# Opening of a fused Fourier-mixing and ELU kernel: which queue brings the filter, and which the weights

## The chip, the cores and the metric

The kernel runs on one core of one Trainium2 chip. The metric is the device time of one execution in microseconds, the median of several runs. Before the change it was 2671.48 us (three runs, 2666.98 to 2671.87).

## The reference

Two blocks follow each other. The first mixes the sequence by a filter in the frequency domain, the second is a two-layer feed-forward with ELU:

```python
# x (8, 3008, 256); filt_r, filt_i (1505, 256); float32
X = np.fft.rfft(x, axis=1)
y = np.fft.irfft(X * (filt_r + 1j * filt_i)[None], n=3008, axis=1).astype(np.float32)
# w_in (256, 2048), w_out (2048, 256): float64
h = y.reshape(24064, 256) @ w_in
g = np.where(h > 0, h, np.exp(np.minimum(h, 0)) - 1)
out = (g @ w_out).astype(np.float32)
```

## The kernel before, in words

**The transform.** The length is 3008 = 47 x 64. For each of the eight batches the transform goes through 64-point stages (`a_unit`, with twiddle tables `ta`), 47-point stages (`b_unit`, table `gb`), a product with the filter on VectorE (L320 to L323), and the way back: 47 points (`bi_unit`, tables `gr` and `gi`) and 64 points (`n_unit`, tables `tn`). Between stages the data goes through DRAM (`z`, `yd`) so that another axis comes to lie on the partitions. `bi_unit` works on eight groups of frequencies, g = 0 to 7; its results are written to `yd` by `y_write` and read again by `y_read`.

**The feed-forward.** `up_steps` and `down_steps` multiply with blocks of the weights, combined in the manner of Strassen and Winograd with seven products instead of eight; `combine` (L394 to L397) makes the sums of the activations on VectorE. One item is a batch, one of six row groups m and one of four quarters q of the 2048 hidden units. These items fill TensorE for most of the span. While items of one batch run, the transform of the next one is laid in between by a plan of places (`plan`, `at`).

**The order of the work** is written by hand (`manual_schedule`): each engine runs its instructions in the order of the program text. Transfers issued by SyncE (`nc.sync`) go by one queue, those issued by GpSimd (`nc.gpsimd`) by another; on an engine whose instruction waits, all later ones wait too.

**The opening** (L641 to L720) is what the change is about. Batch 0 and the weights have no earlier work to hide behind, so this part has its own functions.

- `x_load_first(c)`, L232: for each of six chunks c, the upper half of x comes by SyncE's queue, the mirrored lower half by GpSimd's, and a piece of the forward table `tf` by SyncE's.
- `w_fetch(k)`, L554: the weights are float64, 16 pieces of 512 KB, all on GpSimd's queue. Pieces 4q and 4q+1 are of w_in, 4q+2 and 4q+3 of w_out. There is no room for all raw pieces at once: they lie in buffers that belong to the later pipeline or that the opening has used (6 to 9 in the tiles of x chunks 0 to 3, 10 and 11 in those of chunks 4 and 5, 12 to 14 in the buffers of pieces 1, 2 and 5, and 15 in that of piece 6).
- `w_split(k)` (VectorE), `w_float(k)` (four instructions on ScalarE) and `w_join(k)` (VectorE) make float32 values of the two 32-bit halves of each number. `w_join` of an odd piece also makes the four sums for the Strassen form (L618 to L621). `tick(k)` is `w_float(k)` and then `w_join(k - 1)`. Two sets of temporary tiles are used in turn.
- `a_first(c)`, L239: 16 matrix products and four copies by ScalarE for each chunk, with `w_split(c)` and `w_float(c)` ahead of them in the loop of L677.
- `t_first(g)`, L254: transposes on TensorE with the table `eye`, and copies by ScalarE. Groups 0 to 3 are done right behind the loop; the others in the loop of L695.
- `f_read_first(ff, c)`, L288: the filter in the order the products want, from rows 64 KB apart, in 11 transfers for each of the real and the imaginary part. Elements are 1 and 2 KB. The real part goes by SyncE's queue, the imaginary part by GpSimd's behind chunk 2 (L684). The tile `ff` holds all eight groups.
- The loop of L695: in step g the units `bi_unit(0, g - 2)` and `b_unit(0, g)`, and, if `TICKS` names a piece for the step, its `w_split` ahead of them and its `tick` behind:

```python
TICKS = {0: 7, 1: 8, 2: 9, 3: 10, 4: 11, 5: 12, 7: 13, 8: 14, 9: 15}
```

In the last step `y_write` and `y_read` bring the first row group, then come `w_join(15)` (L713), the loads of the next batch and `n_unit(0, 0)` (L720), from which the items start.

Of the kernel before, what the change touches and what calls it, by code (L numbers as in the profile page):

```python
# [25 lines left out]
P = 128  # L26
D = 256
# [13 lines left out]
def _make_tables():  # L41

    n2, k2 = np.arange(N2), np.arange(K2)
    ta, tn = np.zeros((P, H, P)), np.zeros((P, H, P))
    for i in range(H):
        for h in range(2):
            if h and i == 0:
                continue
            n1 = N1 - i if h else i  # L60
            th = 2 * np.pi * (((N1 * n2[:, None] + n1) * k2[None]) % N) / N
            c, s = np.cos(th), -np.sin(th)
            c[:, 0], s[:, 0] = 1.0, 1.0 - 2.0 * (n2 % 2)
# [36 lines left out]
    gf = np.zeros_like(gb)  # L100
    for o in (0, 64):
        gf[o:o + 48] = gb[o:o + 48].reshape(2, H, 2, 64).swapaxes(0, 1).reshape(48, 2, 64)
    return [t.astype(np.float32) for t in (ta, tn, gb, gr, gi, tf, np.eye(P), gf)]


def order(m):
# [5 lines left out]
def kernel(  # L112
# [8 lines left out]
):  # L121
    nc = tc.nc

    ta_d, tn_d, gb_d, gr_d, gi_d, tf_d, eye_d, gf_d = [
        nc.inline_tensor(t, name=n + "_t").ap()
        for t, n in zip(_make_tables(), ("ta", "tn", "gb", "gr", "gi", "tf", "eye", "gf"))
    ]

    def pool(name, bufs, **kw):
# [17 lines left out]
    psO = pool("psO", 1, space=PSUM)  # L147
    psM = pool("psM", 1, space=PSUM)

    gb, gr, gi = (glob.tile([P, 2, 64], FP32, name=n) for n in ("gb", "gr", "gi"))  # L150

    w_in, w_out = ([glob.tile([P, 7, 2, P], FP32, name="%s%d" % (n, i)) for i in range(4)] for n in ("wi", "wo"))

# [63 lines left out]
    def x_place_first(c):  # L217
        if c < XBUFS:
            t = xp.tile([P, 2, 2, D], FP32, tag="xc", name="xc").rearrange("p k u d -> p (k u) d")
        else:  # L220
            t = t1p.tile([P, XC, D], FP32, tag="t1", name="x1")
        if c < 2:
            w = tnp.tile([P, 4, P], FP32, tag="tn", name="tn")
        else:
            if c % 2 == 0:
                tas["pair"] = t4p.tile([P, 4, D], FP32, tag="t4", name="t0").rearrange("p u (w f) -> p (u w) f", f=P)
            w = tas["pair"][:, 4 * (c % 2):4 * (c % 2) + 4, :]
        xs[0, c], tas[0, c] = t, w
        if c == 0:
            nc.vector.memset(t[HALVES[1], 0, :], 0.0)  # L230

    def x_load_first(c):  # L232
        t = xs[0, c]
        u = 1 if c == 0 else 0
        nc.sync.dma_start(t[HALVES[0]].rearrange("p u d -> p (u d)"), raw(x, XC * c, [[N1 * D, 64], [1, XC * D]]))
        nc.gpsimd.dma_start(t[HALVES[1], u:XC, :], raw(x, N1 - XC * c - u, [[N1 * D, 64], [-D, XC - u], [1, D]]))
        nc.sync.dma_start(tas[0, c], tf_d[:, 4 * c:4 * c + 4, :])

    def a_first(c):  # L239
        xt, w = xs.pop((0, c)), tas.pop((0, c))  # L240
# [44 lines left out]
        for a, r in enumerate((LO, HI)):  # L285
            nc.gpsimd.dma_start(t[r].rearrange("p c u d -> p (c u d)"), fd[g, a].rearrange("q c u d -> q (c u d)"))

    def f_read_first(t, c):  # L288


        src, queue = ((filt_r, nc.sync), (filt_i, nc.gpsimd))[c]
        for a in ((0, 1), (1, 0))[c]:
            r = a * 64
            queue.dma_start(t[r:r + 48:2, :, c, :, :].rearrange("q g u d -> q g (u d)"),
                            raw(src, 2 * a, [[64 * D, 24], [4 * D, NG], [1, 2 * D]]))
            for u in range(2):
                g0 = 1 if a == u == 0 else 0
                for j, n in ((0, 16), (16, 7)):
                    queue.dma_start(t[r + 1 + 2 * j:r + 2 * (j + n):2, g0:NG, c, u, :],
                                    raw(src, 64 * (j + 1) - 4 * g0 - 2 * a - u,  # L300
                                        [[64 * D, n], [-4 * D, NG - g0], [1, D]]))
            if a == 0:
                queue.dma_start(t[1:48:2, 0, c, 0, :], raw(src, 32, [[64 * D, 24], [1, D]]))

    def tile_mm(ps, table, k, rhs, special):
        for u, w, v in ((0, 1, 1), (1, 1, 0)) if special else ((0, 2, 0),):
# [244 lines left out]

    wds = {}

    def w_fetch(k):  # L554
        q, j = divmod(k, 4)

        if k in (3, 4):
            wd = t2p.tile([P, 4, D], FP32, tag="t2", name="wd").rearrange("p u d -> p (u d)")
        elif k in (10, 11):
            wd = t1p.tile([P, XC, D], FP32, tag="t1", name="wd").rearrange("p u d -> p (u d)")  # L560
        elif k in (6, 7, 8, 9, 15):
            wd = xp.tile([P, 2, 2, D], FP32, tag="xc", name="wd").rearrange("p k u d -> p (k u d)")
        else:
            wd = fbufs[{5: 0, 12: 1, 13: 2, 14: 0}.get(k, k)].rearrange("p c u d -> p (c u d)")
        wd = wds[k] = wd.bitcast(U32).rearrange("p (a w) -> p a w", w=2)
        if j < 2:
            srcs = [moe_w_in.bitcast(U32)[ts(j, P), ts(q, 1024)]]
        else:
            srcs = [moe_w_out.bitcast(U32)[ts(4 * q + 2 * (j - 2) + i, P), :] for i in range(2)]
        for i, s in enumerate(srcs):  # L570
            n = 512 // len(srcs)
            nc.gpsimd.dma_start(wd[:, ts(i, n), :].rearrange("p a w -> p (a w)"), s)

# [67 lines left out]
    with tc.manual_schedule():  # L641


        TICKS = {0: 7, 1: 8, 2: 9, 3: 10, 4: 11, 5: 12, 7: 13, 8: 14, 9: 15}
        with tc.tile_pool(name="boot", bufs=1) as bp:
            ff = bp.tile([P, NG, 2, 2, D], FP32, name="ff")
            eye = bp.tile([P, P], FP32, name="eye")
            gf = bp.tile([P, 2, 64], FP32, name="gf")
            pq = [bp.tile([P, 2, D], FP32, name="pq%d" % i) for i in range(2)]
            zt[0] += [bp.tile([P, 16 * ROWS], FP32, name="zt%d" % i) for i in range(2)]  # L650

            for z in zt[0] + zt[1]:
                nc.gpsimd.memset(z.rearrange("p (k r) -> p k r", r=ROWS)[:, :, 48:64], 0.0)
            for c in range(NXC):
                x_place_first(c)
            for c in range(NXC):
                x_load_first(c)
                if c < 5:
                    w_fetch(c)
            nc.scalar.memzero(ff[:, 0:NG // 2])  # L660
            nc.vector.memset(ff[:, NG // 2:NG], 0.0)
            wtmp.append([kp.tile([P, 512], U32, tag=t, name=n) for t, n in (("k0", "wm"), ("k1", "we"))] +
# [3 lines left out]
                        [t1p.tile([P, XC, D], FP32, tag="t1", name="wfl").rearrange("p (a b) d -> p a (b d)", a=2)])  # L666
            for i, v in enumerate((1151.0 * 2 ** 23, 255.0 * 2 ** 23)):
                nc.vector.memset(edges[:, i:i + 1], v)
            for t, d in ((gr, gr_d), (gi, gi_d), (gf, gf_d), (eye, eye_d)):
                nc.sync.dma_start(t, d)  # L670
            f_read_first(ff, 0)

            def tick(k):
                w_float(k)
# [2 lines left out]
            for c in range(NXC):  # L677
# [2 lines left out]
                a_first(c)  # L680
                if c > 0:
                    w_join(c - 1)
                    w_fetch(c + 4)
                if c == 2:  # L684
                    f_read_first(ff, 1)
            for k in range(NXC + 4, 14):
                w_fetch(k)
            for g in range(4):
                t_first(g)
            w_split(NXC)  # L690
            tick(NXC)
            w_fetch(14)
            nc.sync.dma_start(gb, gb_d)
            tn_read(0, 0)
            for g in range(NG + 2):  # L695
                k = TICKS.get(g)
# [11 lines left out]
                    y_read(0, 0, (nc.sync, nc.scalar))  # L708
                if k:
                    tick(k)  # L710
                if g == 0:
                    w_fetch(15)
        w_join(15)  # L713
        for c in range(2):
            x_load(1, c)
# [102 lines left out]
```

## Time and profile before

The span of the profiled execution is 2667.6 us. From the page:

| engine | busy us | share |
|---|---|---|
| TensorE (PE) | 2597.2 | 97% |
| TensorE weight load (PEld) | 2209.1 | 83% |
| VectorE (DVE) | 1843.3 | 69% |
| ScalarE (ACT) | 1508.7 | 57% |
| GpSimd (POOL) | 248.0 | 9% |

Stretches of the opening, from the view of busy time by stage:

| us | PE busy | VectorE busy | ScalarE busy | TensorE clock | DMA share | GB/s |
|---|---|---|---|---|---|---|
| 10 to 30 | 10.97 | 11.43 | 15.44 | 0.83 | 1.04 | 286 |
| 34 to 48 | 8.75 | 6.20 | 9.75 | 0.76 | 1.03 | 172 |
| 50 to 60 | 0.00 | 0.77 | 2.53 | 0.50 | 1.05 | 284 |

Busy times are sums over the stretch. The clock is what the throttle granted TensorE, as a share of full speed, and the DMA share is the mean over the core's 16 DMA engines. In the traffic views, "q1 hardware_dynamic" is the queue of SyncE, "q0 software_dynamic" that of GpSimd; the columns are packets, MB and the time of the packets as a share of 16 engines' span. Each GpSimd transfer from the ninth on is issued only when the one eight before it has landed, so the timeline of its issues also tells landings. The last landings that VectorE's first product (L320, at 63.69 us) could have waited for are those of the filter.

### The profile page before, as it was taken

How to read it: one execution, taken by the hardware profiler on the slowest of the kernel's cores; microseconds unless marked ns; L12 is line 12 of the kernel's file. 1: busy time of each engine (PE TensorE's matmuls, PEld its weight loads, DVE VectorE, ACT ScalarE, POOL GpSimd, SP SyncE). 2: the span in 40 equal slices, each digit the busy share in tenths (PEclk: the TensorE clock that was granted, in tenths of full speed). 3: DMA queues.
4: the chain of work that ended last, by engine and by line, in shares of the span. 5: the costliest groups of instructions: out<-in, count | busy, mean ns of one | idle time of the engine just before them, and what ended most of it. 6: DMA issues, size and time to landing. Idle time of an engine off the chain costs nothing.

```text
span 2667.6 us, 37278 instructions
## 1 busy us (share of the span) xinstructions
PE 2597.2 (97%) x13508; PEld 2209.1 (83%) x13508; DVE 1843.3 (69%) x3203; ACT 1508.7 (57%) x2622; POOL 248.0 (9%) x300
## 2 busy tenths in 40 slices
PE   4799999999999999999999999999999999999998
PEld 3488789888898878988889878898789887898887
DVE  4876767677676776667766676676767677666665
ACT  5655555555555555555555555555555555555554
POOL 3031200012000120002100021001210011000000
PEclk7899999999999999999999999999999999999999
DMA  9464311443124331333214242134321333110110
GB/s 243 114 132 111 102 44 38 102 105 86 38 57 121 80 79 40 95 86 86 74 39 102 74 103 69 38 87 104 99 52 39 78 83 80 38 40 19 23 26 16
DMA packets 229832, 202.87 MB, mean 76 GB/s; under 512 B 132952, under 2 KB 196107, under 8 KB 229649
## 3 DMA queue, kind: packets, MB, share of 16 engines
q1 hardware_dynamic: 211889, 163.33, 24.9%
q0 software_dynamic: 17456, 36.70, 5.6%
q8 instruction: 107, 1.75, 0.3%
q14 instruction: 76, 0.62, 0.1%
q10 hardware_dynamic: 304, 0.46, 0.1%
HBM read 128.45 MB, written 74.97 MB: 76 GB/s over the span
## 4 chain that ended last, share of the span: by engine, by line
PE 94%; DVE 2%; DMA 2%; issue 1%; ACT 0%; SPq 0%; DVEq 0%
PE po L501 43%; PE phs L419 25%; PE phd L419 12%; PE pha L419 6%; PE psn L371 3%; PE pva L308 2%; PE psr L308 2%; PE psa L206 2%; DMA ff<-in_filt_r_dram 1%; DMA x<-in_x_dram 1%; DVE si L321 0%; DVE sr L320 0%; PE pvb L308 0%; DVE wfl L603 0%; DVE we L601 0%
## 5 line engine op out<-in xcount | busy, mean ns | idle before, releaser
L501 PE MATMUL po<-g,wo 128*128 128x256 f32 (+1 forms) x5376 | 1296.7, 375 | 0.0
L501 PEld LDWEIGHTS po<-g,wo 128*128 128x128 f32 x5376 | 1015.0, 190 | 129.5 <-issue 16.2
L430 ACT ACTIVATE g<-phs 128x512 f32<-128x512 f32 (+1 forms) x576 | 339.1, 589 | 842.8 <-PE phs L419 842.1
L427 DVE TENSOR_TENSOR g<-phd,g 128x512 f32<-128x512 f32 (+1 forms) x384 | 259.6, 676 | 463.8 <-ACT e L437 278.0
L437 ACT ACTIVATE e<-e 128x512 f32<-128x512 f32 (+1 forms) x768 | 477.3, 621 | 24.4
L419 PE MATMUL phs<-y,wi 128*128 128x256 f32 (+1 forms) x1536 | 394.8, 379 | 0.0
L419 PE MATMUL phs<-ys,wi 128*128 128x256 f32 (+1 forms) x1536 | 387.6, 375 | 1.5 <-ACT g L430 1.5
L441 DVE SCALAR_TENSOR_TENSOR g<-e,g 128x512 f32<-128x512 f32 (+1 forms) x576 | 387.1, 672 | 0.2 <-ACT e L437 0.2
L436 ACT ACTIVATE e<-g 128x512 f32<-128x512 f32 (+1 forms) x576 | 352.8, 612 | 35.4 <-DVE g L427 29.3
L419 PEld LDWEIGHTS phs<-y,wi 128*128 128x128 f32 x1536 | 284.5, 190 | 83.1 <-ACT t L340 34.1
L419 PEld LDWEIGHTS phs<-ys,wi 128*128 128x128 f32 x1536 | 291.4, 190 | 35.3 <-ACT g L430 2.2
L441 DVE SCALAR_TENSOR_TENSOR g<-e,phs 128x512 f32<-128x512 f32 (+1 forms) x192 | 129.9, 677 | 139.3 <-ACT e L437 139.3
L419 PE MATMUL phd<-ys,wi 128*128 128x256 f32 (+1 forms) x768 | 193.9, 375 | 1.8 <-DVE g L427 1.8
L419 PE MATMUL pha<-y,wi 128*128 128x256 f32 (+1 forms) x768 | 193.8, 375 | 0.0
L419 PE MATMUL phd<-y,wi 128*128 128x256 f32 (+1 forms) x768 | 193.7, 375 | 0.0
L436 ACT ACTIVATE e<-phs 128x512 f32<-128x512 f32 (+1 forms) x192 | 113.0, 588 | 141.6 <-PE phs L419 140.7
L329 POOL TENSOR_TENSOR sr<-sr,sp 128x512 f32<-128x512 f32 x56 | 71.2, 1272 | 1242.8 <-DVE sp L322 1242.8
L419 PEld LDWEIGHTS phd<-ys,wi 128*128 128x128 f32 x768 | 145.7, 190 | 18.9 <-DVE g L427 2.5
L419 PEld LDWEIGHTS pha<-y,wi 128*128 128x128 f32 x768 | 145.8, 190 | 16.8 <-ACT y L373 0.2
L419 PEld LDWEIGHTS phd<-y,wi 128*128 128x128 f32 x768 | 145.8, 190 | 16.5
L481 DVE TENSOR_TENSOR g<-g,g 128x512 f32<-128x512 f32 (+1 forms) x192 | 130.7, 681 | 6.7
L478 DVE TENSOR_TENSOR g<-g,g 128x512 f32<-128x512 f32 (+1 forms) x192 | 130.7, 681 | 6.6
(142 smaller groups left out, 2396.0 us busy)
## 6 DMA issues: line engine op xcount, KB each, us to landing
yd<-t SPq DMA_DIRECT2D x127, 192.0 KB
t<-yd SPq DMA_DIRECT2D x190, 128.0 KB
z<-t SPq DMA_DIRECT2D x84, 256.0 KB
f<-fd POOLq DMA_DIRECT2D x112, 192.0 KB, 3.7
t<-z SPq DMA_DIRECT2D x224, 96.0 KB
out_dram<-o SPq DMA_DIRECT2D x640, 32.0 KB
tn<-tn_t SPq DMA_DIRECT2D x48, 256.0 KB
xc<-in_x_dram SPq DMA_DIRECT2D x84, 128.0 KB
```

Source lines behind the costliest of these rows:

```text
L308: nc.tensor.matmul(ps[:, u:u + w, :], table[k, v, :], r[k, u:u + w, :], start=n == 0, stop=n == len(rhs) - 1)
L329: nc.gpsimd.tensor_tensor(out=sr, in0=sr, in1=p, op=ALU.add)
L371: nc.tensor.matmul(ps[:, ts(q, P)], t[:, i - 4 * m, ds(dh * P, P)], w[:, i - 4 * m, :], start=True, stop=True)
L419: nc.tensor.matmul(ps[:, a, 0:h], w_in[q][:, COMBO[n], a, :], y[n], start=start and a == 0, stop=True, skip_group_check=True)
L427: nc.vector.tensor_tensor(out=g[o], in0=i0, in1=i1, op=ALU.add)
L430: nc.scalar.activation(out=g[o], in_=i0, func=AXT.Copy)
L436: nc.scalar.activation(out=e, in_=src, func=AXT.Relu, scale=-1.0)
L437: nc.scalar.activation(out=e, in_=e, func=AXT.Exp, scale=-1.0)
L441: nc.vector.scalar_tensor_tensor(out=g[n], in0=es[n], scalar=1.0, in1=src, op0=ALU.subtract, op1=ALU.max)
L478: nc.vector.tensor_tensor(out=b12, in0=b22, in1=b12, op=ALU.subtract)
L481: nc.vector.tensor_tensor(out=g["t4"], in0=g["b21"], in1=g["t2"], op=ALU.subtract)
L501: nc.tensor.matmul(po[i][:, u, 0:h], w_out[q][:, COMBO[n], a, :], g[n][:, a, :], start=q == 0 and a == 0 and n in (1, 3, 6, 4), stop=True, ...
```

## The change

It rearranges what comes by which queue in the opening, and when. GpSimd's queue brings the lower half of x for all six chunks, then the whole filter, then weight pieces 8 to 15. SyncE's queue brings piece 0, the upper half of x with the tables `tf` and pieces 1 to 4 in between, the table `once` (which merges `eye` and `gf`), pieces 5 to 7, and the table `gs` (which merges `gb`, `gr` and `gi`). From chunk 2 on, `tf` is loaded for two chunks at a time. The conversions move as well: pieces 6 and 7 are both done ahead of the loop over the groups, 8 to 14 in steps 0, 1, 3, 5, 7, 8 and 9, and 15 behind it. It is meant to bring the filter before the products ask for it, and to take its small elements off SyncE's queue.

```diff
-    ta_d, tn_d, gb_d, gr_d, gi_d, tf_d, eye_d, gf_d = [
+    ta_d, tn_d, gs_d, tf_d, once_d = [
...
-    gb, gr, gi = (glob.tile([P, 2, 64], FP32, name=n) for n in ("gb", "gr", "gi"))
+    gs = glob.tile([P, 3, 2, 64], FP32, name="gs")
+    gb, gr, gi = (gs[:, i] for i in range(3))
...
-        nc.sync.dma_start(tas[0, c], tf_d[:, 4 * c:4 * c + 4, :])
+        if c < 2:
+            nc.sync.dma_start(tas[0, c], tf_d[:, 4 * c:4 * c + 4, :])
+        elif c % 2 == 0:
+            nc.sync.dma_start(tas.pop(("pair", c // 2)), tf_d[:, 4 * c:4 * c + 8, :])
...
-    def f_read_first(t, c):
-        src, queue = ((filt_r, nc.sync), (filt_i, nc.gpsimd))[c]
-        for a in ((0, 1), (1, 0))[c]:
-            r = a * 64
-            queue.dma_start(...)
+    def f_read_first(t):
+        for a, c in ((0, 0), (1, 1), (0, 1), (1, 0)):
+            r, src = a * 64, (filt_r, filt_i)[c]
+            nc.gpsimd.dma_start(...)
...
-    def w_fetch(k):
+    def w_fetch(k, queue=nc.gpsimd):
...
-        TICKS = {0: 7, 1: 8, 2: 9, 3: 10, 4: 11, 5: 12, 7: 13, 8: 14, 9: 15}
+        TICKS = {0: 8, 1: 9, 3: 10, 5: 11, 7: 12, 8: 13, 9: 14}
...
+            w_fetch(0, nc.sync)
             for c in range(NXC):
                 x_place_first(c)
             for c in range(NXC):
                 x_load_first(c)
-                if c < 5:
-                    w_fetch(c)
+                if 0 < c < 5:
+                    w_fetch(c, nc.sync)
...
-            for t, d in ((gr, gr_d), (gi, gi_d), (gf, gf_d), (eye, eye_d)):
-                nc.sync.dma_start(t, d)
-            f_read_first(ff, 0)
+            nc.sync.dma_start(once, once_d)
+            f_read_first(ff)
...
                 if c > 0:
                     w_join(c - 1)
-                    w_fetch(c + 4)
-                if c == 2:
-                    f_read_first(ff, 1)
+                    w_fetch(c + 4, nc.sync if c < 4 else nc.gpsimd)
+            nc.sync.dma_start(gs, gs_d)
             for k in range(NXC + 4, 14):
                 w_fetch(k)
             for g in range(4):
                 t_first(g)
-            w_split(NXC)
-            tick(NXC)
-            w_fetch(14)
-            nc.sync.dma_start(gb, gb_d)
+            for k in (NXC, NXC + 1):
+                w_split(k)
+                tick(k)
+                w_fetch(k + 8)
...
                 if k:
                     tick(k)
-                if g == 0:
-                    w_fetch(15)
+            w_split(15)
+            tick(15)
         w_join(15)
```

More of the change, by code (lines that the diff above doesn't have):

```diff
@@ L102, in _make_tables @@
         gf[o:o + 48] = gb[o:o + 48].reshape(2, H, 2, 64).swapaxes(0, 1).reshape(48, 2, 64)
-    return [t.astype(np.float32) for t in (ta, tn, gb, gr, gi, tf, np.eye(P), gf)]
+    once = np.stack([np.eye(P), gf.reshape(P, P)], 1)
+    return [t.astype(np.float32) for t in (ta, tn, np.stack([gb, gr, gi], 1), tf, once)]
 def order(m):
@@ L122 @@
     nc = tc.nc
-    ta_d, tn_d, gb_d, gr_d, gi_d, tf_d, eye_d, gf_d = [
+    ta_d, tn_d, gs_d, tf_d, once_d = [
         nc.inline_tensor(t, name=n + "_t").ap()
-        for t, n in zip(_make_tables(), ("ta", "tn", "gb", "gr", "gi", "tf", "eye", "gf"))
+        for t, n in zip(_make_tables(), ("ta", "tn", "gs", "tf", "once"))
     ]
@@ L225, in x_place_first @@
             if c % 2 == 0:
-                tas["pair"] = t4p.tile([P, 4, D], FP32, tag="t4", name="t0").rearrange("p u (w f) -> p (u w) f", f=P)
-            w = tas["pair"][:, 4 * (c % 2):4 * (c % 2) + 4, :]
+                tas["pair", c // 2] = t4p.tile([P, 4, D], FP32, tag="t4", name="t0").rearrange("p u (w f) -> p (u w) f", f=P)
+            w = tas["pair", c // 2][:, 4 * (c % 2):4 * (c % 2) + 4, :]
         xs[0, c], tas[0, c] = t, w
@@ L286, in f_read @@
             nc.gpsimd.dma_start(t[r].rearrange("p c u d -> p (c u d)"), fd[g, a].rearrange("q c u d -> q (c u d)"))
-    def f_read_first(t, c):
-        src, queue = ((filt_r, nc.sync), (filt_i, nc.gpsimd))[c]
-        for a in ((0, 1), (1, 0))[c]:
-            r = a * 64
-            queue.dma_start(t[r:r + 48:2, :, c, :, :].rearrange("q g u d -> q g (u d)"),
-                            raw(src, 2 * a, [[64 * D, 24], [4 * D, NG], [1, 2 * D]]))
+    def f_read_first(t):
+        for a, c in ((0, 0), (1, 1), (0, 1), (1, 0)):
+            r, src = a * 64, (filt_r, filt_i)[c]
+            nc.gpsimd.dma_start(t[r:r + 48:2, :, c, :, :].rearrange("q g u d -> q g (u d)"),
+                                raw(src, 2 * a, [[64 * D, 24], [4 * D, NG], [1, 2 * D]]))
             for u in range(2):
@@ L298, in f_read_first @@
                 for j, n in ((0, 16), (16, 7)):
-                    queue.dma_start(t[r + 1 + 2 * j:r + 2 * (j + n):2, g0:NG, c, u, :],
-                                    raw(src, 64 * (j + 1) - 4 * g0 - 2 * a - u,
-                                        [[64 * D, n], [-4 * D, NG - g0], [1, D]]))
+                    nc.gpsimd.dma_start(t[r + 1 + 2 * j:r + 2 * (j + n):2, g0:NG, c, u, :],
+                                        raw(src, 64 * (j + 1) - 4 * g0 - 2 * a - u,
+                                            [[64 * D, n], [-4 * D, NG - g0], [1, D]]))
             if a == 0:
-                queue.dma_start(t[1:48:2, 0, c, 0, :], raw(src, 32, [[64 * D, 24], [1, D]]))
+                nc.gpsimd.dma_start(t[1:48:2, 0, c, 0, :], raw(src, 32, [[64 * D, 24], [1, D]]))
     def tile_mm(ps, table, k, rhs, special):
@@ L571, in w_fetch @@
             n = 512 // len(srcs)
-            nc.gpsimd.dma_start(wd[:, ts(i, n), :].rearrange("p a w -> p (a w)"), s)
+            queue.dma_start(wd[:, ts(i, n), :].rearrange("p a w -> p (a w)"), s)
     wts, wtmp = {}, []
@@ L641 @@
     with tc.manual_schedule():
-        TICKS = {0: 7, 1: 8, 2: 9, 3: 10, 4: 11, 5: 12, 7: 13, 8: 14, 9: 15}
+        TICKS = {0: 8, 1: 9, 3: 10, 5: 11, 7: 12, 8: 13, 9: 14}
         with tc.tile_pool(name="boot", bufs=1) as bp:
             ff = bp.tile([P, NG, 2, 2, D], FP32, name="ff")
-            eye = bp.tile([P, P], FP32, name="eye")
-            gf = bp.tile([P, 2, 64], FP32, name="gf")
+            once = bp.tile([P, 2, P], FP32, name="once")
+            eye, gf = once[:, 0], once[:, 1].rearrange("p (v q) -> p v q", v=2)
             pq = [bp.tile([P, 2, D], FP32, name="pq%d" % i) for i in range(2)]
```

## The prediction

> **What bounds the kernel now.** I read the busy row of the page first: TensorE works 97% of the span. So a change to the opening can only move the moment from which that steady work runs. Four stretches, in the view of busy time by stage, show where that moment lies (columns: stretch, length, then busy time and count of PE, PEld, DVE, ACT, POOL, then TensorE clock, DMA share, GB/s):
>
> ```profile
> 0.00:63.69 63.69, 25.13 (x156) 22.14 (x156) 26.02 (x53) 36.02 (x66) 24.17 (x47) 0.78 0.99 249
> 63.69:104.56 40.87, 35.55 (x195) 13.96 (x196) 39.76 (x78) 26.16 (x46) 1.60 (x3) 0.85 0.29 80
> 104.56:117.36 12.80, 2.18 (x15) 0.70 (x14) 9.61 (x21) 6.56 (x11) 0.00 (x0) 0.73 0.52 128
> 117.36:2667.60 2550.24, 2534.36 (x13144) 2172.28 (x13144) 1767.86 (x3054) 1439.93 (x2500) 222.26 (x250) 1.00 0.29 71
> ```
>
> To 63.69 the 16 DMA engines are full (0.99) and no compute engine is. From there to 104.56 VectorE is full (39.76 of 40.87 us): eight filter products and the weight pieces between them. Then comes a chain of waits, and from 117.36 TensorE is full to the end. The change touches the first three stretches only. The chain of waits names what ends the first and the third (start, length, what):
>
> ```profile
> 25.98 22.95 DMA ff<-in_filt_r_dram
> 48.95 4.77 DMA ff<-in_filt_r_dram
> 53.73 9.77 issue
> ...
> 63.69 0.49 DVE sr L320
> ...
> 110.01 3.06 DMA yd<-t
> ...
> 113.59 3.69 DMA t<-yd
> ...
> 117.36 3.55 PE psn L371 x16
> ```
>
> VectorE's first product waits for the filter tile ff. The 9.77 us "issue" is, I take it, the landing of SyncE's last filter transfer, issued in the group 37.50 to 49.71. The traffic of three stretches says why it is late (bytes and engine time of each queue; q1 is SyncE's, q0 GpSimd's), here 10 to 15, 34 to 48 and 50 to 60 us:
>
> ```profile
> q0 software_dynamic: 251, 0.87, 61.2%
> q1 hardware_dynamic: 252, 0.60, 43.3%
> ```
> ```profile
> q0 software_dynamic: 615, 1.33, 55.3%
> q1 hardware_dynamic: 829, 1.06, 46.5%
> ```
> ```profile
> q0 software_dynamic: 660, 2.28, 83.2%
> q1 hardware_dynamic: 528, 0.55, 21.8%
> ```
>
> At 10 to 15 us the queues send the same number of packets. At 50 to 60 SyncE's queue has 1 KB filter packets against 4 KB weight packets and gets 0.55 MB of 2.84. At 34 to 48 both carry filter, and all 16 engines move only 172 GB/s against 284 to 294. Engine time per KB: 0.612 x 80 / 870 = 56 ns for weights and x; 0.218 x 160 / 550 = 63 ns for filter beside weights; 0.553 x 224 / 1330 = 93 and 0.465 x 224 / 1060 = 98 ns with filter on both.
>
> [...]without the packets under 512 B (half of them put to each queue), q0's filter packets at 34 to 48 are 1330 KB / 431 = 3.1 KB, q1's 1060 / 645 = 1.6 KB. [...]
>
> **The change, part by part.** All filter transfers go behind the x halves on GpSimd's queue, where they are packed larger and met by SyncE's traffic. But SyncE's queue now has, in one line, half of x, the twiddles (tf), weight pieces 0 to 7 and the tables. In ScalarE's program the conversion of piece 5 (w_float) stands before the last copies of a_first(5), so t_first waits for that whole line. I work out the moment S, the first product on VectorE (63.69 now), from bytes.
>
> First stretch: 1.51 MB of x on GpSimd's queue, 384 packets; SyncE's 384 packets beside it are w0, x0, tf0, x1 = 1.31 MB. 2.82 MB x 57 ns / 16 = 10.0 us. The 0.75 MB moved in the first 5 us put the start at 2.4; so it ends at 12.4.
>
> Second: the filter, 3.08 MB, about 1000 packets. Its cost per KB is not in the trace for this mixture, between 63 and 96 ns. Filter takes 22% of engine time where it cost 63 and all of it where it cost 96; here about 53%, so 76 by proportion: 234 engine-us. SyncE sends 1.0 (first traffic view) to 1.5 packets (645/431) for each; I take 1.25, so 1250: tf1, w1, x2, tf2-3, w2, x3, w3, x4, tf4-5 and the first of w4, 3.81 MB (w_out and tf1 as 2 KB rows), x 57 = 217 engine-us. Together 451 / 16 = 28.2: ends at 40.6. The filter is there some 20 us earlier than now.
>
> Third: SyncE still owes the rest of w4, x5, "once" and w5, 1.30 MB. GpSimd's queue now holds w8 and w9 (1.05 MB), whose buffers a_first(2) and (3) have freed; w10 must wait for a_first(4). 2.35 MB x 57 / 16 = 8.4: 49.0. Piece 5 had its bytes across at 30.1 (4.65 MB on q0) and its slot back at 31.5, so add 1.4: w5 lands at 50.4, where it now lands before 32.6.
>
> Then, by rows of now: w5 to the last copy of a_first(5) 4.3 (32.58 to 36.92); t_first's eight copies to 44.20, 7.3; w_float(6) 2.5; and, new ahead of the first product, w_join(6) 2.0 and w_split(8) 0.7. Now only w_split(7) stands there. Sum 16.8: **S = 67.2**, 3.5 us later. Behind the waiting split and join stand all eight products, and TensorE's bi_unit behind these. w6, w7 and gs follow w5 and are needed 10 to 18 us after it; the filter and w8 are there: hidden.
>
> After S: eight products of 2.40 (4 x 0.60) stay. Two joins and two splits leave the stretch up to the last product. Step by step, now 5.10, 6.77, 5.00, 6.70, 5.15, 6.10, 3.67 = 38.5 from first to last. Then: 6.75 (odd join 3.65, split 0.68), 4.4, about 4.0 (TensorE's transposes, bi_unit and b_unit bind, no join there), 6.05, 3.65, 4.4, 3.67 = 32.9. Saved 5.6. Given back: w_join(11), an odd one, stands ahead of the split that ScalarE's last copy waits for, 1.65; and three joins end behind that chain rather than two, so combine (L394) starts 5.4 instead of 2.9 us after n_unit, and the third up step needs its result: 2.5, minus about 0.8 in how the chain meets it. Net gain after S: 5.6 - 1.65 - 1.75 = 2.2. The x halves' order and the merged tables (three issues fewer of 0.32) lie beside full DMA engines: nothing.
>
> Sum: + 3.5 - 2.2 = **+ 1.3 us**, 2671.5 + 1.3 = 2672.8.
>
> **Rivals.** *SyncE's line is faster than I think, and it gains.* Filter at 63 ns: - 40 engine-us, 2.5 us. GpSimd's queue short of packets: in the timeline its issues wait for landings 8 transfers back (24.51 to 39.02), so SyncE may send two packets for one, and w8, w9 fall behind w5: - 3.7. S = 61.0; with the late combine hidden too (1.7), 61.0 - 63.7 - 3.9 = - 6.6: about 2665. For it: 829 packets against 615, on a queue with just such filter transfers. [...]
> *The slow mixture slows both.* At 34 to 48 both queues paid over 90. If filter costs 96 and SyncE's packets 80 beside it, the second stretch takes (296 + 305) / 16 = 37.6, + 9.4: 2682. For it: q1's and q0's cost rose together. Against: weights beside filter cost 58 at 50 to 60.
> *TensorE's clock drops.* It is 0.50 at 50 to 60, after idling, and 0.76 at 34 to 48. a_first's units spread over 50 us instead of 37, so t_first may run at 0.5 to 0.6: 7.3 becomes 10 to 11: about 2676. This adds to any case.
>
> **How the numbers follow.** Within 0.2% (2666.1 to 2676.8) is the likeliest case, 0.38: two large moves cancel. Faster 0.33: the first rival and mixtures of its terms; S has only to come to 60.5, or to 62 with the combine hidden. Slower 0.29: the second and third. With both ends of the unknown costs the range is 2659 to 2682.
>
> **What would show it.** Right: filter landed by 40 to 46 with VectorE still waiting; the last a_first copies at 52 to 57; S at 65 to 70; SyncE's packets 1 to 1.5 for each of GpSimd's; n_unit near 117. Wrong: a_first(5) before 48, S before 61 (first rival), under 220 GB/s while the filter moves (second), or steps of products still 5 us apart without a join.

## The result and the profile after

The changed kernel takes 2679.56 us (median of four runs, 2678.52 to 2683.34), the kernel before beside it on the same chip 2670.86 us. The ratio is 1.0038, with an interval of 1.002 to 1.0055: slower by some 9 us. The profiled execution spans 2677.1 us against 2667.6.

The view of busy time by stage of the changed kernel, in the four stretches of the prediction (up to the first product, up to the end of the last, up to the first normalisation, the rest; columns as there):

```profile
0.00:70.51 70.51, 29.93 (x156) 26.83 (x156) 28.76 (x58) 36.18 (x67) 24.80 (x48) 0.80 0.93 231
70.51:110.47 39.96, 35.89 (x195) 14.91 (x196) 33.22 (x63) 22.96 (x42) 0.52 (x1) 0.76 0.26 70
110.47:125.60 15.13, 2.19 (x15) 0.70 (x14) 12.39 (x28) 8.15 (x15) 0.00 (x0) 0.72 0.50 122
125.60:2677.10 2551.50, 2535.36 (x13144) 2173.16 (x13144) 1769.58 (x3057) 1440.87 (x2502) 222.32 (x250) 1.00 0.29 71
```

Line by line against before: + 6.82, - 0.91, + 2.33 and + 1.26, together + 9.5, the whole difference of the spans. In the second stretch VectorE does 6.5 us less (33.22 after 39.76), and the stretch is hardly shorter: it waits instead. DMA moves 231 GB/s up to the first product where it moved 249.

The chain of waits of the changed kernel, in order of time (start, length, what):

```profile
7.98 21.09 DMA f<-in_moe_w_out_dram
...
32.15 23.77 DMA f<-in_moe_w_in_dram
...
59.53 4.98 PE po L268 x31
...
67.43 4.46 issue
...
117.62 2.98 DMA yd<-t
...
121.09 4.27 DMA t<-yd
125.60 3.75 PE psn L374 x16
```

Where the filter stood (ff), weight pieces stand: the chain runs through pieces on SyncE's queue until 55.9 us (the last is piece 5), then through the transposes of `t_first`. The tail from the last product on has the same links as before, later.

The traffic of the changed kernel at 20 to 45 us (filter on q0, weights and x on q1) and at 53 to 60 (weight pieces and a table, hardly any filter); columns are packets, MB, share of 16 engines:

```profile
DMA packets 2196, 5.16 MB, mean 206 GB/s; under 512 B 608, under 2 KB 685, under 8 KB 2196
q1 hardware_dynamic: 1199, 3.01, 61.1%
q0 software_dynamic: 997, 2.14, 44.6%
```
```profile
DMA packets 1097, 2.76 MB, mean 394 GB/s; under 512 B 149, under 2 KB 262, under 8 KB 1097
q0 software_dynamic: 496, 1.71, 63.4%
q1 hardware_dynamic: 601, 1.04, 40.8%
```

While the filter moves, both queues pay dearly: 0.611 x 400 / 3010 = 81 ns of engine time per KB on q1, 0.446 x 400 / 2140 = 83 on q0. With hardly any of it, 0.634 x 112 / 1710 = 42 and 0.408 x 112 / 1040 = 44. All 16 engines are full in both (the shares add to 106 and 104%).

VectorE's timeline of the changed kernel shows what this does to the opening (start, length, instruction, idle time before it and what ended that):

```profile
49.19 0.43 DVE L587 TENSOR_SCALAR wm<-wd 128x512 uint32<-128x512 uint32 x1 [7.96 <-DMA wd<-in_moe_w_in_dram]
...
55.94 0.43 DVE L587 TENSOR_SCALAR wm<-f 128x512 uint32<-128x512 uint32 x1 [2.28 <-DMA f<-in_moe_w_in_dram]
...
67.83 0.69 DVE L604 SCALAR_TENSOR_TENSOR we<-wd,we 128x512 uint32<-128x512 uint32 x1 [2.88 <-ACT we L598]
...
69.84 0.42 DVE L587 TENSOR_SCALAR wm<-wd 128x512 uint32<-128x512 uint32 x1
...
70.51 0.68 DVE L323 TENSOR_TENSOR sr<-psr,ff 128x512 f32<-128x512 f32 x1
```

The line at 49.19 is the split of piece 4, that at 55.94 the split of piece 5, at the landing of its bytes. At 67.83 the join of piece 6 starts after its last `w_float`, at 69.84 the split of piece 8, and then the first product. This is the path that the prediction laid, 3.3 us later than it said.

### The profile page after: what moved, and what is told of

Its sections match the earlier page's. It is cut to its first block, busy times and chain, and to the rows that moved or that the text cites. A ratio compares the mean times of both kernels' runs of the same rounds, so it can differ in the third digit from the quotient of the medians.

```text
span 2677.1 us, 37269 instructions
## 1 busy us (share of the span) xinstructions
PE 2603.4 (97%) x13508; PEld 2215.6 (83%) x13508; DVE 1844.0 (69%) x3203; ACT 1508.2 (56%) x2622; POOL 247.6 (9%) x299
## 3 DMA queue, kind: packets, MB, share of 16 engines
q8 instruction: 107, 1.75, 0.3%
## 4 chain that ended last, share of the span: by engine, by line
PE 95%; DMA 2%; DVE 1%; ACT 0%; issue 0%; DVEq 0%; ACTq 0%; SPq 0%
PE po L504 42%; PE phs L422 25%; PE phd L422 12%; PE pha L422 6%; PE psn L374 3%; PE pva L311 2%; PE psr L311 2%; PE psa L208 2%; DMA f<-in_moe_w_in_dram 1%; DMA f<-in_moe_w_out_dram 1%; PE pvb L311 0%; PE po L268 0%; DMA xc<-in_x_dram 0%; PE psi L311 0%; DMA t<-yd 0%
```

## Experiments

Each kernel was timed beside the kernel before on the same chip. The median of the latter was 2668.6 to 2670.9 us there, and its single executions lay between 2664.6 and 2674.3. So one trace, which shows a single execution, can lie some 5 us off the median: times are medians, and traces are read for mechanisms and rates.

### The moved conversions and the moved queues, each alone

The kernel before, with only the conversions' order of the changed kernel:

```diff
-        TICKS = {0: 7, 1: 8, 2: 9, 3: 10, 4: 11, 5: 12, 7: 13, 8: 14, 9: 15}
+        TICKS = {0: 8, 1: 9, 3: 10, 5: 11, 7: 12, 8: 13, 9: 14}
...
-            w_split(NXC)
-            tick(NXC)
-            w_fetch(14)
+            for k in (NXC, NXC + 1):
+                w_split(k)
+                tick(k)
+                w_fetch(k + 8)
...
-                if g == 0:
-                    w_fetch(15)
+            w_split(15)
+            tick(15)
```

> The kernel before with only the order of the conversions as in the changed kernel (pieces 6 and 7 ahead of the loop over the groups, 15 behind it); queues and tables stay. Theory A (SyncE's line through piece 5 delays the first product; the conversions' order costs little): the filter still sets the first product at about 63.7 us, the moved join and split lie in the wait for it, and the stretch behind it gets a few us shorter, less what the late joins give back: 2667 to 2672 us. Rival B (the moved conversions are what costs): first product 2 to 3 us later and a longer tail, 2674 to 2678 us.

Measured: 2670.18 us, ratio 1.0004 (0.9996 to 1.0012): no difference. VectorE's timeline of its trace has the split of piece 8 and the first product as in the first two lines below. The third line is the first product of another kernel with the old queues and with pieces 6 and 7 ahead of the loop, the one with late joins under "Two tries at the tail":

```profile
56.92 0.43 DVE L584 TENSOR_SCALAR wm<-wd 128x512 uint32<-128x512 uint32 x1 [0.94 <-DMA wd<-in_moe_w_in_dram]
...
57.67 0.69 DVE L320 TENSOR_TENSOR sr<-psr,ff 128x512 f32<-128x512 f32 x1
```
```profile
62.49 0.69 DVE L320 TENSOR_TENSOR sr<-psr,ff 128x512 f32<-128x512 f32 x1 [6.28 <-issue]
```

In the third line the two conversions lie in the wait for the filter, with 6.28 us to spare (6.70 in the other try at the tail). The trace of the order alone, of its fastest execution (2665.96 us), shows another case: the filter had landed earlier, the split of piece 8 waited for its own bytes, and the first product came 6.0 us before the 63.69 of the kernel before. Of these, 3.2 us were lost again behind the last product, from which on the span takes 2566.2 us there and 2563.0 before. How often either case occurs is not known from single traces; the median is unmoved.

And the changed kernel with these lines undone, so that only queues and tables differ from before:

> The changed kernel with the order of the conversions as before; queues and tables as changed. Theory A: piece 5 still lands near 56 us, the last a_first copies come at 59.7, t_first's at 65.3; the first product needs no join of piece 6 any more and comes at about 65.5 instead of 70.5; the stretch behind it is as long as before the change: 2673 to 2676 us. Rival B: the whole loss goes, 2669 to 2672 us. Rival C (TensorE at half clock stretches the steps): the gain of 5 us at the first product is mostly eaten, 2677 to 2680 us.

Measured: 2671.97 us, ratio 1.0011 (1.0004 to 1.0018). Its stages, in the stretches from its own first product on:

```profile
0.00:64.36 64.36, 26.05 (x144) 24.03 (x148) 26.13 (x53) 31.19 (x59) 23.47 (x46) 0.71 1.01 243
64.36:105.23 40.87, 36.30 (x211) 14.54 (x204) 39.77 (x79) 30.51 (x54) 1.60 (x3) 0.87 0.31 85
105.23:118.22 12.99, 2.18 (x15) 0.69 (x14) 9.80 (x21) 6.55 (x11) 0.00 (x0) 0.77 0.52 131
118.22:2669.20 2550.98, 2534.82 (x13144) 2172.83 (x13144) 1768.07 (x3054) 1439.92 (x2500) 222.00 (x250) 1.00 0.29 71
```

The second stretch has the 40.87 us of before, to the digit. Against the changed kernel the four lines differ by 6.15, - 0.91, 2.14 and 0.52: the conversions' order costs 7.9 us here (7.6 by the medians), most of it in the first line. Piece 5 was split at 54.91 instead of 55.94, so 5.1 of the 6.15 are the conversion of one more piece ahead of the first product. Under the old queues the same order cost nothing. So the loss is a product of two edits: the queues alone cost 1 to 5 us, the order alone nothing, both together 5 to 15.

### Why the filter's traffic is slow: pitch, element size, mixture

The filter's rows lie 64 KB apart. The same transfers from rows 61 KB apart (other filter numbers, so another output):

```diff
-                                raw(src, 2 * a, [[64 * D, 24], [4 * D, NG], [1, 2 * D]]))
+                                raw(src, 2 * a, [[61 * D, 24], [4 * D, NG], [1, 2 * D]]))
```

(and the like in the other two transfers)

> The changed kernel with the filter read from rows 61 KB apart instead of 64 KB: same number, size and destinations of elements, but rows that are not the filter's for these groups, so the product is with other numbers. If reads at a power-of-two pitch are what slows both queues to 206 GB/s while the filter moves: over 260 GB/s there, piece 5 lands some 5 to 7 us earlier, first product at 64 to 66, 2672 to 2675 us. If the small elements or their few destination partitions are it: nothing moves, piece 5 at 55 to 57, 2678 to 2681 us.

Measured: 2677.86 us, ratio 1.0033 (1.0021 to 1.0046), 207 GB/s at 20 to 45 us. The pitch is not the cause. The same bytes to the same partitions in elements of 8 and 16 KB (other numbers again):

```diff
-            nc.gpsimd.dma_start(t[r:r + 48:2, :, c, :, :].rearrange("q g u d -> q g (u d)"),
-                                raw(src, 2 * a, [[64 * D, 24], [4 * D, NG], [1, 2 * D]]))
+            nc.gpsimd.dma_start(t[r:r + 48:2, 4 * c:4 * c + 4].rearrange("q g c u d -> q (g c u d)"),
+                                raw(src, 2 * a, [[16 * D, 24], [1, 16 * D]]))
```

(and the like in the other transfers)

> The changed kernel with the filter's transfers in elements of 16 and 8 KB instead of 2 and 1 KB, to the same 24, 16 and 7 partitions: about the same bytes, same queue; the products are with other numbers. If small elements are the cause of the slow traffic: 250 to 285 GB/s between 20 and 45 us, piece 5 at 47 to 51, 2671 to 2675 us. If few destination partitions are: no change, piece 5 at 54 to 57, 2676 to 2680 us. (From pitch: the rows at 61 KB moved nothing, so an effect of the changed addresses is not expected.)

Measured: 2680.93 us, ratio 1.0039 (1.0027 to 1.0052), 215 GB/s. At 20 to 45 us, 243 of its 1767 packets have 8 KB or more, and none of the changed kernel's, so the packets did grow with the elements; element size is not the cause either. All weight pieces back on GpSimd's queue, behind the filter:

```diff
-            w_fetch(0, nc.sync)
...
-                if 0 < c < 5:
-                    w_fetch(c, nc.sync)
+                if c < 5:
+                    w_fetch(c)
...
-                    w_fetch(c + 4, nc.sync if c < 4 else nc.gpsimd)
+                    w_fetch(c + 4)
```

> The changed kernel with all weight pieces on GpSimd's queue again: 0 to 4 between the x halves, then the whole filter, then 5 and on. Theory A (what counts is the line that holds piece 5): ahead of piece 5 on its queue lie 7.2 MB where SyncE's line had 5.9, but SyncE's queue is empty early and the filter then has the engines alone; piece 5 lands at 46 to 52, first product at 61 to 67, 2670 to 2676 us. If only the sum of bytes ahead counts: piece 5 lands near 55 as now, 2677 to 2680 us.

Measured: 2677.42 us, ratio 1.0029 (1.0018 to 1.0041); piece 5 split at 54.2 and the first product at 68.8. At 40 to 50 us only GpSimd's queue moves anything, nearly all of it filter. Its traffic then:

```profile
DMA packets 643, 1.44 MB, mean 144 GB/s; under 512 B 280, under 2 KB 280, under 8 KB 643
q0 software_dynamic: 643, 1.44, 90.3%
```

0.903 x 160 / 1440 = 100 ns per KB with nothing beside it. The filter's transfers are slow by themselves, and this other order of queues did not mend that.

### Why it is slow: where the rows go

What is left is the destination. A filter transfer goes to 24, 16 or 7 partitions. Here to 96, 64 or 28, with the same bytes and element sizes (other numbers):

```diff
-            nc.gpsimd.dma_start(t[r:r + 48:2, :, c, :, :].rearrange("q g u d -> q g (u d)"),
-                                raw(src, 2 * a, [[64 * D, 24], [4 * D, NG], [1, 2 * D]]))
+            nc.gpsimd.dma_start(t[0:96, 2 * a:2 * a + 2, c, :, :].rearrange("q g u d -> q g (u d)"),
+                                raw(src, 2 * a, [[8 * D, 96], [4 * D, 2], [1, 2 * D]]))
```

(and the like in the other transfers)

> The changed kernel with the filter's transfers sent to four times as many partitions: same bytes but for a few KB, same queue, same element sizes (2 and 1 KB), 96, 64 and 28 partitions instead of 24, 16 and 7; the products are with other numbers. In the changed kernel 206 GB/s were moved while the filter ran (20 to 45 us), and about 80 ns of engine time per KB were paid on both queues. If few destination partitions are the cause: 250 to 285 GB/s there, piece 5 lands at 47 to 51 instead of 56, first product at 62 to 66, 2671 to 2675 us. If small elements are: no change, piece 5 at 54 to 57, 2676 to 2680 us.

Measured: 2672.82 us, ratio 1.0013 (1.0007 to 1.002), 242 GB/s, piece 5 split at 49.4 and the first product at 63.9. The source rows moved as well here, but other source rows alone had changed nothing (61 KB apart, and the long elements). So the destination is the cause; but by what: the number of partitions, an uneven share of the 16 engines (24 and 7 do not divide by 16), or which partitions? First 16 adjacent partitions to every transfer (other numbers):

```diff
+            nc.gpsimd.dma_start(t[16 * i:16 * i + 16, 0:6, :, :, :].rearrange("q g c u d -> q (g c) (u d)"),
+                                raw(src, 2 * a, [[64 * D, 16], [4 * D, 12], [1, 2 * D]]))
             for u in range(2):
+                for p, g, n in ((64 + 16 * a, 0, 8), (96, 4 * a, 4)):
+                    nc.gpsimd.dma_start(t[p:p + 16, g:g + n, c, u, :],
+                                        raw(src, 2 * a + u, [[64 * D, 16], [4 * D, n], [1, D]]))
```

(`i` counts the four passes of the loop)

> The changed kernel, with every filter transfer of the opening to exactly 16 partitions (same element sizes, same bytes within 2%, each tile row a source row of its own; the product then runs on other filter numbers, so the output is not the reference's). The run with 96/64/28 partitions moved 242 GB/s between 20 and 45 us, had the first product at 63.9 and 2672.8 us. Two readings of it: (a) what is slow is an uneven spread of a transfer over the 16 DMA engines (24 and 7 rows don't divide by 16): then 16 rows are as good as 96, 235 to 245 GB/s, first product 63 to 66, 2671 to 2674 us. (b) what is slow is a transfer to few partitions, however even: then 16 rows are no better than 24, 195 to 215 GB/s, first product 68 to 72, 2677 to 2681 us.

Measured: 2684.45 us, ratio 1.0059 (1.0045 to 1.0072), 177 GB/s. Neither reading had said this: even transfers, and slower than the changed kernel's uneven ones. That rules out the uneven share and points to which partitions. So the same transfers once more, with the 16 partitions 8 apart (the lines are against the kernel just shown; p is 0, 4, 1 and 5 in turn, and the like in the other transfers):

```diff
-            nc.gpsimd.dma_start(t[16 * i:16 * i + 16, 0:6, :, :, :].rearrange("q g c u d -> q (g c) (u d)"),
+            nc.gpsimd.dma_start(t[p:p + 121:8, 0:6, :, :, :].rearrange("q g c u d -> q (g c) (u d)"),
                                 raw(src, 2 * a, [[64 * D, 16], [4 * D, 12], [1, 2 * D]]))
```

> As the run with 16 adjacent partitions to a filter transfer (177 GB/s between 20 and 45 us, first product at 76.2 us, 2684.5 us), the same bytes, element sizes and 16 partitions, but these lie 8 apart (0, 8, ... 120 and so on) instead of side by side (other filter numbers again). [...] Theory[...]: as in the changed kernel or a little better, 200 to 230 GB/s, first product 65 to 71, 2674 to 2680 us. Rival, that the number of partitions sets it: as with 16 adjacent ones, 170 to 185 GB/s, first product 74 to 78, 2682 to 2687 us.

and with 32 partitions 4 apart (p is 0 or 1, h is 0 or 3, and the like in the other transfers):

```diff
+            nc.gpsimd.dma_start(t[p:p + 125:4, h:h + 3, :, :, :].rearrange("q g c u d -> q (g c) (u d)"),
+                                raw(src, 2 * a, [[46 * D, 32], [4 * D, 6], [1, 2 * D]]))
```

> The same with 32 partitions 4 apart to each filter transfer (same bytes and element sizes, other filter numbers): [...]with a third of the partitions of the run with 96/64/28 ([...]242 GB/s, first product 63.9, 2672.8 us). Theory[...]: at least as fast as that one, 240 to 265 GB/s, first product 60 to 64, 2669 to 2673 us. Rival, number of partitions: between the changed kernel's 24 and the 96, 206 to 225 GB/s, first product 67 to 71, 2675 to 2680 us.

Measured: 2674.83 us, ratio 1.0019 (1.0012 to 1.0025), first product at 65.3; and 2666.24 us, ratio 0.9983 (0.9976 to 0.999), first product at 55.5. The traffic at 20 to 45 us of three of these kernels, first 16 adjacent partitions, then 16 that lie 8 apart, then 32 that lie 4 apart:

```profile
DMA packets 1746, 4.43 MB, mean 177 GB/s; under 512 B 384, under 2 KB 416, under 8 KB 1746
q0 software_dynamic: 836, 2.23, 54.1%
q1 hardware_dynamic: 910, 2.21, 50.9%
```
```profile
DMA packets 2404, 6.19 MB, mean 248 GB/s; under 512 B 524, under 2 KB 675, under 8 KB 2404
q1 hardware_dynamic: 1318, 3.28, 55.2%
q0 software_dynamic: 1086, 2.91, 49.5%
```
```profile
DMA packets 3206, 8.44 MB, mean 338 GB/s; under 512 B 599, under 2 KB 759, under 8 KB 3206
q1 hardware_dynamic: 1775, 4.24, 54.1%
q0 software_dynamic: 1431, 4.20, 49.9%
```

The first two differ in nothing but which 16 partitions: 97 ns per KB on q0 (0.541 x 400 / 2230) against 68, and on q1, which carries weights and x in both, 92 against 67. The engines are equally full in all three (the shares of the two queues add to 104 or 105%). So number and engines are not it. The third, with 32 partitions, beats the kernel with 96, 64 and 28: number is not it again. Its 338 GB/s is flattered, though: behind the filter, GpSimd's queue issues 3 MB of weight pieces within these 25 us. At 20 to 30 us, where q0 carries filter in all of them, the three move 170, 247 and 304 GB/s, the changed kernel 226 and the one with 96, 64 and 28 partitions 248.

Which property of the set of partitions decides is not shown. The number of partitions does not order these rates, and neither does the distance between them: 96, 64 and 28 side by side move 248 GB/s at 20 to 30 us, 16 that lie 8 apart 247, and 16 side by side 170. The rates are mixtures with q1's traffic, and even the higher rates expected of the last two kernels (200 to 230 and 240 to 265) were too low. Shown is that the choice of partitions alone moves the rate from 170 to 247 (177 to 248 at 20 to 45 us).

The last kernel runs on other filter numbers, so it is no version to use. A layout of `ff` with 32 partitions 4 apart would have to be matched in the order in which `b_unit`'s tables put out the frequencies; that was not tried.

### The steps of the products and TensorE's clock

A step is the time from the first of the four products of one group to that of the next. The prediction had the third and the sixth at 4.0 and 4.4 us; the changed kernel has 5.93 and 6.70. Its timeline of the two engines in the sixth step, TensorE first, then VectorE:

```profile
99.30 1.33 PE L311 MATMUL pva<-sr,gs 48*64 48x512 f32 x2 [1.70 <-ACT t L343]
...
100.42 1.06 PE L311 MATMUL pva<-sp,gs 48*64 48x512 f32 x1
...
104.93 0.59 PE L311 MATMUL pva<-pq,gs 48*64 48x512 f32 x1
```
```profile
101.35 0.76 DVE L617 TENSOR_TENSOR wo<-wfl,we 128x256 f32<-128x256 f32 x2
104.33 0.69 DVE L323 TENSOR_TENSOR sr<-psr,ff 128x512 f32<-128x512 f32 x1 [2.21 <-PE psi L311]
```

TensorE waits 1.70 us for ScalarE's copy. Its granted clock is 1.00 at 98 to 100 us and 0.50 at 100 to 102, and its matmuls then take 1.06 us instead of 0.59. VectorE is done with its join and waits 2.21 us. To see whether a warm TensorE would shorten the steps, 40 transposes without a use were put ahead of the first `bi_unit`:

```diff
+                if g == 2:
+                    ps = psO.tile([P, 2, 256], FP32, name="po2")
+                    for i in range(40):
+                        nc.tensor.transpose(ps[0:ROWS, 0, 0:P], zt[0][0][:, ts(i % 16, ROWS)], eye)
```

> The changed kernel with 40 extra transposes on TensorE into an unused PSUM tile, in the 4.7 us in which it waits ahead of the first bi_unit. Theory C (TensorE comes back from that wait at half clock, and so the steps without a join stay long): the granted clock between 72 and 86 us rises from 0.50 to 0.9 or more, the steps of the first products 4.63 and 5.93 become about 4.4 and 4.0, the stretch to the last product shortens by 2 to 4 us: 2674 to 2677 us. If the clock is not what binds the steps, or the extra work does not hold it up: within 1 us of the changed kernel, 2677 to 2680 us.

Measured: 2678.27 us, ratio 1.0032 (1.002 to 1.0045). Its stages at 60 to 72 and in its third step:

```profile
60.00:72.00 12.00, 11.90 (x103) 9.71 (x103) 9.05 (x20) 10.43 (x18) 2.12 (x5) 0.98 0.54 202
80.01:85.95 5.94, 5.94 (x33) 2.75 (x34) 3.15 (x6) 2.02 (x4) 0.00 (x0) 0.63 0.29 64
```

While the transposes ran, the clock was 0.98 (0.78 at 60 to 72 us in the changed kernel), but in the third step it was 0.63 again, as in the changed kernel, and the steps stayed (5.94 and 6.69). The experiment did not reach what it was meant to test. Three runs made for another reason did: with 16 adjacent partitions, with 16 that lie apart and with 32, the third step took 4.93, 4.72 and 4.73 us at granted clocks of 0.76 to 0.79, and the sixth then 7.59, 7.58 and 7.58 at 0.57 to 0.59. Third and sixth together are 12.3 to 12.5 us in them and 12.6 in the changed kernel: what the one step gains, the other loses. The kernel with rows 61 KB apart is alike (4.61 us, then 7.58; granted 0.87 at 80 to 85 us, 0.50 at 95 to 100). So the length of the third step goes with TensorE's clock, but a third step at a better clock brought only 0.1 to 0.4 us over both. What decides when it rises stays open.

### Two tries at the tail

In the tail the combination waits for joins that stand behind the last product. The kernel before with pieces 6 and 7 ahead of the loop as in the changed kernel, piece 13 in the loop's last step, and the joins of pieces 14 and 15 in the first two items of the feed-forward:

```diff
-        TICKS = {0: 7, 1: 8, 2: 9, 3: 10, 4: 11, 5: 12, 7: 13, 8: 14, 9: 15}
+        TICKS = {0: 8, 1: 9, 3: 10, 5: 11, 7: 12, 9: 13}
...
-                if g == 0:
-                    w_fetch(15)
-        w_join(15)
+            w_split(14)
+            tick(14)
+        wtmp[1] = wtmp[0]
...
+        at(0, 0, w_join, 14)
+        at(0, 1, w_split, 15)
+        at(0, 1, w_float, 15)
+        at(1, 0, w_join, 15)
```

> The kernel before with the moved conversions (as in the run with the conversions' order alone), and in addition no conversion of pieces 13 and 14 on ScalarE ahead of the last bi_unit's copies (13 behind y_read), and the joins of 14 and 15 in the first two items of the feed-forward, with one set of temporary tiles. Theory: with the moved conversions the sums of combine start 19.7 us after the last product, as against 15.7 before, because three joins are behind the tail; without these the sums start 13 to 14 us after it. Then 2663 to 2667 us, faster than both kernels. If TensorE waits as long for VectorE's joins inside the first items: no gain, 2668 to 2672 us.

Measured: 2671.88 us, ratio 1.0007 (0.9999 to 1.0016). Its last two stages:

```profile
102.40:112.94 10.54, 2.18 (x15) 0.69 (x14) 7.81 (x18) 5.04 (x10) 0.00 (x0) 0.72 0.68 168
112.94:2669.70 2556.76, 2536.46 (x13144) 2177.01 (x13144) 1773.98 (x3067) 1443.43 (x2507) 221.95 (x250) 1.00 0.29 71
```

The tail is 2.3 us shorter than before (12.80), and the rest 6.5 us longer (2556.76 after 2550.24): at 131.5 TensorE waits 4.90 us at one stretch for ScalarE's activation g, which stands behind the moved conversion. The other try has pieces 6 and 7 ahead of the loop, and eight in it:

```diff
-        TICKS = {0: 7, 1: 8, 2: 9, 3: 10, 4: 11, 5: 12, 7: 13, 8: 14, 9: 15}
+        TICKS = {0: 8, 1: 9, 2: 10, 3: 11, 4: 12, 5: 13, 7: 14, 9: 15}
```

> The kernel before, with its queues and tables, pieces 6 and 7 converted ahead of the filter product and the other eight at items 0,1,2,3,4,5,7 and 9, none behind the combination (the run with the changed order alone had 7.58 us in its sixth step and 19.7 us from the last product to the combination). Theory: the two conversions ahead lie in the wait for the filter, and with only join 14 or 15 behind the last product, the first normalisation's matmuls start 10 to 11 us and the combination 13 to 14 us after the last product instead of 12.8 and 15.7; steps of 6.8 5.1 5.0 6.7 5.1 4.4 3.7; 2666 to 2668.5 us beside about 2670 of before. Rival: the tail's gain is taken back by TensorE's waits behind the combination, or the opening's first product comes later by what the two conversions cost: 2669.5 to 2672 us, no different from before.

Measured: 2668.57 us beside 2668.64, ratio 0.9999 (0.9991 to 1.0007). Its stretches of products and tail:

```profile
61.98:104.20 42.22, 38.30 (x195) 15.91 (x196) 39.72 (x77) 25.79 (x45) 0.52 (x1) 0.69 0.30 86
104.20:114.62 10.42, 2.21 (x15) 0.72 (x14) 6.97 (x16) 4.25 (x8) 0.00 (x0) 0.69 0.61 156
```

The tail is as worked out (10.42, with 10 to 11 expected). But the products take 42.22 us where they took 40.87, with the same work of VectorE (39.72 us after 39.76): 1.35 of the 2.4 us are spent on steps that waited longer (TensorE's clock is 0.69 there, 0.85 before). What remains is within the spread. No run gave a usable version faster than the kernel before.

## Why the prediction missed its size

The time lies inside the range (2659 to 2682), and slower was among the cases, at 0.29; the likeliest was no difference, + 1.3 us. The range was 23 us wide because it took both ends of the unknown costs, so that the time lies in it says little for the sum. The path was right in its links; two terms were mis-sized, by 8 us together. Of the signs named for being right, the first product at 65 to 70 and the last copies of `a_first` at 52 to 57 were missed narrowly, at 70.5 and 59.7.

**The prices of the second stretch (3.3 us net).** The step that failed took 76 ns per KB for the filter and left SyncE's packets at 57, "Its cost per KB is not in the trace for this mixture". They were 83 and 81. That is the second rival (80 beside 96), whose mark was "under 220 GB/s while the filter moves": 206. On 3.81 MB of SyncE's and 3.08 MB of filter the difference is 3810 x 24 + 3080 x 7 = 113 us summed over the 16 DMA engines, or 7.1 us; piece 5 came 5.5 us later than said (55.9 for 50.4). I had taken the price of one queue's packets as its own property, and weighted only the filter's. But the runs with 16 partitions show q1's price moving with q0's destination (92 to 67).

As a number the second rival was off both ways. It had the first product 9.4 us later than the main forecast, where the prices came to 7.1 and piece 5 to 5.5; the copies and transposes behind piece 5 then took less than the terms taken from before (3.7 us to the last copy of `a_first`, 4.3 said; 5.7 for `t_first`, 7.3 said); and it knew nothing of the steps below. The third rival, `t_first` of 10 to 11 us at a low clock, did not come about.

**The conversions ahead of the first product: right.** 2.5 + 2.0 + 0.7 = 5.2 us were said to be new on the path; undoing them gave 5.1. That they are hidden as long as the filter is the last to land is shown by the two tries at the tail (waits of 6.28 and 6.70 us behind them).

**The steps (4.7 us).** The seven steps said, 6.75, 4.4, about 4.0, 6.05, 3.65, 4.4 and 3.67, came as 6.77, 4.63, 5.93, 6.05, 3.73, 6.70 and 3.74. Five of seven are right to 0.25 us, and the saving of 5.6 became 0.9. The third was said to be bound by TensorE, and was, but at a granted clock of 0.63; the sixth was worked out as VectorE's sum, and it waited for TensorE, which had waited for a copy of ScalarE. Removing VectorE's work from a step paid only up to the next engine's time here, and that engine's time was taken at full clock.

**Given back: right in sum.** 1.65 + 1.75 = 3.4 were said, 2.33 + 1.26 = 3.6 measured.

**The filter** itself was no longer last, as said, but late: its last transfer is issued at 43.9 us and lands 9.9 us later, at 53.8, long after 40 to 46 (DMA moves 221 GB/s at 45 to 52 us, and 394 only from 53 on). It is hidden behind piece 5.

## What to carry to other kernels

By the partitions that it writes, a transfer can make the others beside it slow too (92 ns per KB on q1 beside 16 adjacent partitions, 67 beside 16 that lie 8 apart). Before moving transfers between full queues, ask which partitions each one writes, since that set the rate here (170 to 304 GB/s at 20 to 30 us), while pitch (206 and 207 GB/s at 20 to 45 us) and element size (206 and 215) did not, and putting the weights back on the other queue brought little (ratio 1.0029 after 1.0038). Work that is free in a wait has a price as soon as the wait is removed (nothing under the old queues here, 7.6 us under the new ones), so a change of transfers and a change of order have to be costed together. And a step from which one engine's work is taken is as long as the next engine's, at the clock that this engine will have after waiting (the third step took 5.93 us for the 4.0 said, with TensorE at 0.63).

## What was not expected of the hardware

- The same kind of transfers, 16 partitions each, differ by 40% or more in rate between adjacent partitions and partitions 8 apart (177 and 248 GB/s at 20 to 45 us, 170 and 247 at 20 to 30), and the other queue's packets slow down with them (92 and 67 ns per KB).
- 1 and 2 KB elements are hardly slower, if at all, than 8 and 16 KB ones in this traffic (206 and 215 GB/s at 20 to 45 us, 226 and 220 at 20 to 30), nor rows 64 KB apart than rows 61 KB apart (206 and 207).
- TensorE's clock rose late here. TensorE's records leave no gap from 71.9 us on in the changed kernel, yet by the view of stages its clock stays at 0.50 up to 86, for 14 us:

```profile
72.00:74.00 2.00, 2.00 (x7) 1.08 (x10) 2.00 (x4) 0.69 (x1) 0.30 (x1) 0.50 0.00 0
...
84.00:86.00 2.00, 2.00 (x12) 0.56 (x10) 1.07 (x3) 0.41 (x1) 0.00 (x0) 0.50 0.03 8
86.00:88.00 2.00, 2.00 (x19) 0.59 (x12) 0.15 (x1) 0.98 (x3) 0.00 (x0) 0.92 0.00 0
```

With 7 to 14 matmuls in 2 us, a record without a gap need not be an array at work; whether these matmuls wait inside their records for data is not shown.
